# First batch of an FFT mixer: the way back to tokens through DRAM instead of through transposes, and three sections of batch 2 ahead of the first unit

## The chip, the cores and the metric

The kernel runs on one core of a Trainium2 chip. The metric is device time in microseconds (us) for one execution of the whole program. The kernel before takes 1328.95 us, the median of 3 runs (1328.45 to 1333.54).

## What is computed

The input x has 4 batches of 3136 tokens with 256 channels. First a filter in the frequency domain runs along the tokens, then two blocks of dense layers:

```python
y = irfft(rfft(x, axis=1) * (filt_r + 1j * filt_i), n=3136, axis=1)
h = (y^T @ U @ V)^T                      # rank 32, along the tokens
u = y + h
r = u + relu(u @ w_ch1) @ w_ch2          # 256 -> 1024 -> 256
n = (r - mean(r)) / sqrt(var(r) + 1e-6) * g_ln
out = r + relu(n @ w2_ch1) @ w2_ch2      # again 256 -> 1024 -> 256
```

All inputs are fp32 and the result is wanted to fp32 accuracy, so each dense product is made of several products of split operands (high and low parts).

## The kernel before

The transform of 3136 = 112 x 28 points is done in two stages of small matmuls with tables, forward, then a multiplication with the filter, then two stages back. The last stage back and the addition of the rank-32 term are made together, in 28 **units** of 448 tokens (`unit(i)`, seven to a batch). A unit reads a tile `wt` with rows of the third stage's result and a tile `ic` with table columns, and leaves 448 tokens, channels on partitions, in the split tiles `ah` and `al`. Units feed 25 **blocks** of 512 tokens. A block has a phase "a" (`m1` at L824, `m2` at L843 to L845: first dense pair) and a phase "b" (`m1` at L824, `m2` at L851, L852: second pair). A phase has 8 steps, each an `m1` of six matmuls and an `m2` of an earlier step. The loop over `steps` (L1211) also calls units when they are due, conversions of weights (`pr`), and pieces of the transform of batches 2 to 4 (the generator `rest`, from step `FFT0` on, first stage not before step `FFT1`).

Batch 1 is transformed on its own ahead of the first step, by the class `First`, with its data in the SBUF tile `big` (channels on partitions). `columns()` works through 14 channel groups of frequencies, one in a turn of its loop: four transposes out of `big` (`psz`, L656), the second stage (`ps2`, L670), the filter (`filtered`, on DVE and, for all groups but one, POOL) and the third stage (`ps3`, L681). That third stage has the data as the stationary operand and a table beside a slice of U as the moving one, 144 columns wide, so its result has channels on partitions: `spill` (ACT) copies it back into `big`, and `project` (DVE) sums up the 32 columns that belong to U. Behind the loop `mixed()` turns that sum by two transposes (L705), and `part(u)` turns the data for unit u by eight transposes (L728) and two copies (ACT, L732 on DVE). For units 0 to 3 (`DIRECT = 4`) the result goes straight into `wt`; for 4 to 6 it is stored to the DRAM tensor `bd[0]` (L734), from which `load_unit` reads it. Parts 0 and 1 run ahead of the first step, parts 2 to 6 in the steps 0, 1, 2, 5 and 6 (`PARTS`).

Batches 2 to 4 go another way (`fft(b)`): the first stage in seven sections (`load1`, `stage1`, L301) with its result in DRAM (`zd`), then for seven groups the second stage, filter and third stage (`back`, L373 and L375), here with the table stationary in 64x64 quarters of the array, so that tokens are on partitions. The result goes to DRAM (`bd`), and the product with U (`pt`, L381) is made by matmuls of its own. A unit of such a batch loads its rows in two halves (`load_unit`, L756) and uses the two-halves form (L801, L806) instead of the form for `DIRECT` units (L786, L788).

The order of the instructions on every engine is the order in which this program writes them. All transfers but a few leave through one queue, SP's, in that order. A transfer on SP waits there until its data and its target are free, and what stands behind it waits too. Each transfer also waits for the one eight places ahead of it to land, since eight completion counters are used in turn.

Of the kernel before, what the change touches and what calls it, by code (L numbers as in the profile page):

```python
# [10 lines left out]
F32 = mybir.dt.float32  # L11
# [28 lines left out]
SLOTS, UAHEAD = 4, 2  # L40
# [4 lines left out]
DIRECT = 4  # L45

PARTS, UPARTS = (0, 1, 2, 5, 6, 8), 10
# [13 lines left out]
def _tables():  # L61
# [75 lines left out]
    parted = np.zeros((2, P, 2, PP))  # L137
    for g in range(2):
        for k in range(2):
            parted[0, g * 64:(g + 1) * 64, k] = d[0, k * 64:(k + 1) * 64]  # L140
            parted[1, g * 64:(g + 1) * 64, k] = d[1 - g, k * 64:(k + 1) * 64]
    turn = np.zeros((P, NM, QT))
    for h in range(2):
# [9 lines left out]
        "c_d32": np.ascontiguousarray(parted.transpose(1, 0, 2, 3).astype(np.float32)),  # L153
# [5 lines left out]
        "c_inv": np.ascontiguousarray(inv.transpose(1, 0, 2).astype(np.float32)),  # L159
# [24 lines left out]
def fft_mixer_kernel(ctx: ExitStack, tc: tile.TileContext, x, U, V, flt, w1, w2, gln, w1b, w2b,  # L184
                     c_fwd32, c_d32, c_e32, c_p32, c_s1, c_s2, c_s3, c_inv, c_half, c_w, out):
# [94 lines left out]

    def fft(b):
# [12 lines left out]
        def stage1(t):  # L294
# [99 lines left out]
        def finish():  # L394
            t = pt.pop(b)
            s = [flat(fp.tile([P, 2, D], F32, tag="xs", name="tt", bufs=2))[0:R].rearrange("p (a q) -> p a q", q=D) for _ in range(2)]
            for a in range(1, 4):
                acopy(s[a // 2][:, a % 2], t[a * R:(a + 1) * R])
            nc.vector.tensor_tensor(out=s[0][:, 0], in0=t[0:R], in1=s[0][:, 1], op=ALU.add)
            nc.vector.tensor_tensor(out=s[1][:, 0], in0=s[1][:, 0], in1=s[1][:, 1], op=ALU.add)  # L400
            nc.vector.tensor_tensor(out=s[0][:, 0], in0=s[0][:, 0], in1=s[1][:, 0], op=ALU.add)
            stack(b, s[0][:, 0].rearrange("p (q k) -> p k q", k=KT))

# [39 lines left out]
        finish()  # L443
        yield 0

    class First:
# [3 lines left out]
        def load(self, conversions):  # L450
# [5 lines left out]
            for j in range(NM // 4):  # L456
# [17 lines left out]
                for _ in range(FETCHES.count(j)):  # L474
# [75 lines left out]
        def u_half(self, h):  # L550
# [8 lines left out]
            ps = outer("pst")  # L559
# [13 lines left out]
        def u_parts(self):  # L573

            held["uh"] = const.tile([P, 2 * SLOTS * (PP + R)], F32, tag="uh", name="uh_sb")[:, :NG * R].rearrange("p (g r) -> p g r", r=R)
# [26 lines left out]

        def columns(self):


            zt, ys, n, w = {}, {}, NCH, PP + R
            d0, d1 = self.d
            self.t = d1[:, 2, 0:KT * 2 * R].rearrange("p (h g r) -> p h g r", h=KT, g=2)
            turns = [self.u_half(h) for h in (1, 0)]

            def slot(i):
                return d1[:, 0:2] if i == 0 else d0[:, i % SLOTS]

            def spill(pvs, i):
                for g, pv in enumerate(pvs):
                    a = (2 * i + g) * PP
                    (acopy if i or g == 0 else nc.vector.tensor_copy)(self.big[:, :, a:a + PP], pv[:, :, :PP])

            def project(pvs, i):
                for g, pv in enumerate(pvs):  # L620
                    acc = self.t[:, :, g]
                    if i == n - 1:
                        nc.vector.tensor_copy(acc, pv[:, :, PP:])
                    else:
                        nc.vector.tensor_tensor(out=acc, in0=pv[:, :, PP:], in1=acc, op=ALU.add)

            def filtered(i, ps):
# [10 lines left out]
                else:  # L638
                    yr = ps_t.tile([P, 512], F32, tag="t", name="yr").rearrange("p (a d) -> p a d", a=2)
# [8 lines left out]
            due = None  # L648
            for j in range(n + BACKL):
                if j < n:  # L650
                    i = n - 1 - j
                    ps = (ps_h if j % 2 else ps_t).tile([P, 512], F32, tag="h" if j % 2 else "t", name="psz")
# [6 lines left out]
                if due:  # L659
                    spill(*due)  # L660
                    project(*due)
                due = None
# [10 lines left out]
                if j >= BACKL:  # L673
                    i = n + BACKL - 1 - j
                    ya = ys.pop(i)
                    pvs = [outer("ps3")[:, :2 * w].rearrange("p (h w) -> p h w", w=w) for g in range(2)]
                    for dh in range(KT):
                        for k in range(2):
                            for g in range(2):
                                gs = slice(g * HALF, (g + 1) * HALF)  # L680
                                nc.tensor.matmul(pvs[g][:, dh], dealt(ya[gs, k], dh), slot(i)[gs, k], start=k == 0, stop=k == 1)  # L681
                    due = pvs, i
# [3 lines left out]
                if j == 1:  # L686
                    for k in range(2):
                        nc.gpsimd.tensor_copy(d0[:, 1:, k, 0:PP], d0[:, 0, k, 0:PP].unsqueeze(1).to_broadcast([P, SLOTS - 1, PP]))
                for i in (n - 1, n - 2) if j == BACKL - 1 else (n + BACKL - UAHEAD - 1 - j,) if BACKL <= j < n + BACKL - UAHEAD else ():
                    acopy(slot(i)[:, :, PP:w], self.uq[:, :, i])  # L690
                yield j
            spill(*due)
            project(*due)

        def mixed(self):

            tt = fp.tile([P, 2, D], F32, tag="xs", name="tt", bufs=2)[:, 0]
            ps = ps_t.tile([P, 512], F32, tag="t", name="pst")
            for dh in range(KT):
                acc = self.t[:, dh]  # L700
                nc.vector.tensor_tensor(out=acc[:, 0], in0=acc[:, 0], in1=acc[:, 1], op=ALU.add)
            yield
            for dh in range(KT):
                acc = self.t[:, dh]
                nc.tensor.transpose(ps[:R, dh * P:(dh + 1) * P], acc[:, 0], ident)  # L705
            yield
            acopy(tt[0:R], ps[:R, :D])
            stack(0, tt[0:R].rearrange("p (k q) -> p k q", k=KT))

        def part(self, u, between=None):  # L710

            m = slice(UW * u, UW * u + UW)
            if u < DIRECT:
                wt[u] = new_unit(u)
            for dh in range(KT):
                ds = slice(dh * P, (dh + 1) * P)
                if u < DIRECT:
# [9 lines left out]
                for k in range(UW):  # L727
                    nc.tensor.transpose(ps[:PP, k * P:(k + 1) * P], v[:, :, UW * u + k], ident)  # L728
# [538 lines left out]
```

## Time and profile before

| | us |
|---|---|
| median of 3 runs | 1328.95 |
| profiled execution | 1325.22 |
| its span, first to last instruction | 1323.4 |
| TensorE (PE) busy | 1305.7 (99%) |
| VectorE (DVE) busy | 800.1 (60%) |
| ScalarE (ACT) busy | 429.1 (32%) |
| GpSimd (POOL) busy | 151.7 (11%) |

The profiled execution lies 3.7 us below the median of the runs and 1.8 us above its own span. A busy PE counts every matmul from its start to its modelled end, and matmuls overlap, so the length of a stretch of PE work is read from the start of one group to the start of the next, not from the sum of durations. [...]

### The profile page before, as it was taken

The page shows a single profiled execution, that of the slowest core. Times are in us where ns is not written, and L with a number is a line of the kernel's source. Part 1 is how long each engine was busy: PE and PEld are TensorE (multiplying, and loading weights), DVE is VectorE, ACT ScalarE, POOL GpSimd, SP SyncE. Part 2 cuts the span into 40 slices and gives each one's busy share as a digit, 9 for nine tenths or more (in the row PEclk, how much of TensorE's full clock was granted, in tenths as well). Part 3 has the DMA queues.
Part 4 walks back from the last instruction along what each step waited for, and adds up shares of the span by engine and source line. Part 5 has one row for each costly group of instructions (what it writes and reads, how often), then busy time and mean ns, then how long its engine had stood idle before and what let it go on. Part 6 is the DMA issues. An engine that isn't in the chain of part 4 may idle for free.

```text
span 1323.4 us, 22450 instructions
## 1 busy us (share of the span) xinstructions
PE 1305.7 (99%) x8606; PEld 1041.8 (79%) x8606; DVE 800.1 (60%) x1643; ACT 429.1 (32%) x857; POOL 151.7 (11%) x133
## 2 busy tenths in 40 slices
PE   9999999999999999999999999999999999999998
PEld 8688678777778787787777877878888888888887
DVE  6867976666565666556655575665555545455454
ACT  4656432333323323223222233232222223222222
POOL 2845520212000001000001010000000000000000
PEclk9999999999999999999999999999999999999999
DMA  8734365675563446344555464422202211210111
GB/s 252 197 101 137 90 190 183 169 197 160 157 207 91 123 124 173 104 136 110 143 164 147 127 170 121 122 70 66 50 20 62 66 32 52 66 49 5 44 49 40
DMA packets 166531, 151.15 MB, mean 114 GB/s; under 512 B 65912, under 2 KB 142568, under 8 KB 166424
## 3 DMA queue, kind: packets, MB, share of 16 engines
q1 hardware_dynamic: 166120, 148.25, 40.4%
q0 software_dynamic: 304, 1.47, 0.5%
q8 instruction: 68, 1.11, 0.4%
q14 instruction: 39, 0.32, 0.1%
HBM read 91.10 MB, written 47.54 MB: 105 GB/s over the span
## 4 chain that ended last, share of the span: by engine, by line
PE 87%; DVE 5%; DMA 3%; POOL 1%; ACT 1%; issue 1%; SPq 1%; POOLq 0%; DVEq 0%; ACTq 0%
PE psh L824 38%; PE pso L851 13%; PE pso L852 7%; PE pso L843 6%; PE pso L844 6%; PE pso L845 6%; PE psu L801 2%; PE ps L301 2%; PE ps L375 1%; PE ps L341 1%; PE psu L806 1%; PE pt L381 1%; DVE hl L828 1%; DMA stg<-v 1%; DMA x<-x 1%
## 5 line engine op out<-in xcount | busy, mean ns | idle before, releaser
L828 DVE SCALAR_TENSOR_TENSOR hl<-psh,hh 128x512 fp32r<-128x512 f32 (+1 forms) x400 | 271.6, 680 | 363.0 <-ACT hh L827 361.8
L827 ACT ACTIVATE hh<-psh 128x512 fp32r<-128x512 f32 (+1 forms) x400 | 235.1, 589 | 655.8 <-PE psh L824 655.6
L851 PE MATMUL pso<-wb,hh 128*128 128x512 f32 x784 | 285.0, 397 | 0.8 <-DVE x L866 0.4
L824 PE MATMUL psh<-ah,wb 128*128 128x512 f32 (+1 forms) x800 | 280.0, 391 | 0.6 <-DVE hl L828 0.6
L852 PE MATMUL pso<-wb,hl 128*128 128x256 f32 x784 | 219.7, 280 | 0.5 <-DVE hl L828 0.5
L824 PEld LDWEIGHTS psh<-ah,wb 128*128 128x128 f32 x800 | 149.7, 188 | 46.4 <-issue 5.7
L851 PEld LDWEIGHTS pso<-wb,hh 128*128 128x128 f32 x784 | 147.3, 188 | 36.3 <-DVE x L866 1.6
L824 PE MATMUL psh<-ah,w1h 128*128 128x512 f32 (+1 forms) x400 | 158.2, 396 | 0.0
L844 PE MATMUL pso<-hl,w2h 128*128 128x512 f32 (+1 forms) x400 | 154.4, 386 | 2.7 <-DVE hl L828 2.7
L843 PE MATMUL pso<-hh,w2h 128*128 128x512 f32 (+1 forms) x400 | 155.8, 390 | 0.4 <-DVE x2t L891 0.3
L824 PE MATMUL psh<-al,wb 128*128 128x512 f32 (+1 forms) x400 | 155.4, 389 | 0.0
L824 PE MATMUL psh<-al,w1h 128*128 128x512 f32 (+1 forms) x400 | 155.2, 388 | 0.0
L852 PEld LDWEIGHTS pso<-wb,hl 128*128 128x128 f32 x784 | 147.9, 189 | 8.3 <-DVE hl L828 0.9
L824 PE MATMUL psh<-ah,w1l 128*128 128x512 f32 (+1 forms) x400 | 154.4, 386 | 0.0
L845 PE MATMUL pso<-hh,w2l 128*128 128x512 f32 (+1 forms) x400 | 154.0, 385 | 0.0
L357 POOL TENSOR_TENSOR xs<-xs,ft 128x512 f32<-128x512 f32 x42 | 56.2, 1337 | 645.6 <-DMA xs<-zc 375.8
L824 PEld LDWEIGHTS psh<-ah,w1h 128*128 128x128 f32 x400 | 75.1, 188 | 22.7 <-issue 4.7
L891 DVE SCALAR_TENSOR_TENSOR x2t<-pso,ln,x2t 128x256 f32<-128x256 f32 x196 | 89.8, 480 | 3.7 <-PE pso L852 0.3
L843 PEld LDWEIGHTS pso<-hh,w2h 128*128 128x128 f32 x400 | 75.1, 188 | 20.5 <-issue 5.4
L844 PEld LDWEIGHTS pso<-hl,w2h 128*128 128x128 f32 x400 | 75.2, 188 | 18.3 <-DVE hl L828 3.9
L824 PEld LDWEIGHTS psh<-ah,w1l 128*128 128x128 f32 x400 | 75.2, 188 | 15.9
L845 PEld LDWEIGHTS pso<-hh,w2l 128*128 128x128 f32 x400 | 75.1, 188 | 15.1
(150 smaller groups left out, 1333.9 us busy)
## 6 DMA issues: line engine op xcount, KB each, us to landing
ft<-flt SPq DMA_DIRECT2D x42, 512.0 KB
xd<-x SPq DMA_DIRECT2D x96, 128.0 KB
x2t<-xd SPq DMA_DIRECT2D x24, 512.0 KB
wt<-bd SPq DMA_DIRECT2D x48, 224.0 KB
out<-x2t SPq DMA_DIRECT2D x84, 128.0 KB
xs<-zc SPq DMA_DIRECT2D x168, 64.0 KB
xt<-x SPq DMA_DIRECT2D x84, 112.0 KB
zd<-ze SPq DMA_DIRECT2D x84, 112.0 KB
```

The lines of the kernel that those rows point to most:

```text
L301: nc.tensor.matmul(pss[j][quarter(h), m * D:(m + 1) * D], ct[rows56(j), 2 * h + m], xs[h][rows56(j), m], start=True, stop=True)
L357: nc.gpsimd.tensor_tensor(out=xs, in0=xs, in1=fi[:, e], op=ALU.mult)
L801: nc.tensor.matmul(pss[h][c * HALF:(c + 1) * HALF, dh, h * spare + m:h * spare + half:UW], t[rows, m, d0:d0 + HALF], ic[rows, m, :], start ...
L824: nc.tensor.matmul(ps[:, :n], w[:, kt, fs], a[:, kt, :n], start=j == 0, stop=j == 3 * KT - 1)
L827: nc.scalar.activation(out=hh[:, :n], in_=ps[:, :n], func=AF.Relu)
L828: nc.vector.scalar_tensor_tensor(out=hl[:, :n], in0=ps[:, :n], scalar=0.0, in1=f32(hh[:, :n]), op0=ALU.max, op1=ALU.subtract)
L843: nc.tensor.matmul(o, wh[:, f, ds], hh[:, :n], start=f == 0, stop=False)
L844: nc.tensor.matmul(o, wh[:, f, ds], hl[:, :n], start=False, stop=False)
L845: nc.tensor.matmul(o, wl[:, f, ds], hh[:, :n], start=False, stop=f == FT - 1)
L851: nc.tensor.matmul(o, hh[:, cs], w, start=f == 0, stop=False, skip_group_check=True)
L852: nc.tensor.matmul(o[:, D:], hl[:, cs], w[:, :D], start=False, stop=f == FT - 1, skip_group_check=True)
L891: nc.vector.scalar_tensor_tensor(out=o, in0=acc[c][:, half * D:(half + 1) * D], scalar=rs[:, c:c + 1], in1=o, op0=ALU.mult, op1=ALU.add)
```

## The change

- The third stage of batch 1 takes the form of the other batches: the table is stationary, in quarters, for two groups at once (`back(p)`, seven calls). Tokens lie on partitions; the product with U is accumulated in `pt[0]` by four matmuls of 32 columns for each call. Two ACT copies bring the result to a free part of `big`, and four transfers store it to `bd[0]`.
- `spill`, `project`, `mixed`, all transposes of `part`, the table copies on POOL (L688) and the slices of U beside the table (L690) go away. The sum over U's rows is finished by `finish(0)`, as for the other batches.
- All seven units of batch 1 load their rows from `bd[0]` and take the two-halves form.
- The transform of batch 2 starts in `columns()` (`FILLJ`): the loads of its first section stand in turn 13, those of the second in turn 14. Between `finish(0)` and unit 0 stand three sections of its first stage (`FILL = 3`), which leave their result in `big`.
- Some tiles move between PSUM banks.

```diff
-SLOTS, UAHEAD = 4, 2
 PACE = 4
 VSTEP = 11
-DIRECT = 4
-
-PARTS, UPARTS = (0, 1, 2, 5, 6, 8), 10
+FILL, FILLJ = 3, 13
+
+WBSTEP, UPARTS = 2, 10
...
-                ze = four(F32, "fev", "ze")
+                ze = first.spare(t, e) if b == 1 and t < FILL else four(F32, "fev", "ze")
...
-            self.d = [const.tile([P, 2 * SLOTS * (PP + R)], F32, tag="uh", name="d32").rearrange("p (s k q) -> p s k q", k=2, q=PP + R),
-                      fp.tile([P, 2 * (D + R)], F32, tag="fev", name="d32", bufs=2).rearrange("p (s q) -> p s q", q=PP + R)]
-            nc.sync.dma_start(self.d[0][:, 0, :, 0:PP], c_d32[:, 0])
-            nc.sync.dma_start(self.d[1][:, 0:2, 0:PP], c_d32[:, 1])
+            self.d = const.tile([P, NG * R], F32, tag="uh", name="d32")[:, :8 * HALF].rearrange("p (v k j q) -> p v k j q", v=2, k=2, j=2)
+            nc.sync.dma_start(self.d, c_d32)
...
+        def bank(self, j, name):
+            return ps_o.tile([P, 512], F32, tag=f"o{j}", name=name, bufs=1)
+        def spare(self, t, e):
+            return self.big[:, e, 512 * t:512 * t + 512]
...
-            def spill(pvs, i):
...
-            def project(pvs, i):
...
-                    yr = ps_t.tile([P, 512], F32, tag="t", name="yr").rearrange("p (a d) -> p a d", a=2)
+                    yr = self.bank(3, "yr").rearrange("p (a d) -> p a d", a=2)
...
-            due = None
+            def back(p):
+                ya = [ys.pop(2 * p + s) for s in range(2)]
+                pss = [self.bank(g, "ps3") for g in range(2)]
+                for s in (1, 0):
+                    for k in range(2):
+                        for g in range(2):
+                            gs = quarter(g)
+                            for h in range(2):
+                                nc.tensor.matmul(pss[g][quarter(h), s * D:(s + 1) * D], self.d[gs, 0 if p or s else 1, k, h], ya[s][gs, k],
+                                                 start=k == 0, stop=k == 1)
+                if p == n // 2 - 1:
+                    pt[0] = ps_t.tile([P, 512], F32, tag="t", name="pt")[:, :D]
+                for s in (1, 0):
+                    for k in range(2):
+                        q = 2 * s + k
+                        nc.tensor.matmul(pt[0][q * R:(q + 1) * R], self.uq[:, k, 2 * p + s], ya[s][:, k], start=p == n // 2 - 1, stop=p == 0)
+                to = bd[0].rearrange("(j a s g p) w -> a g j p s w", j=2, a=n // 2, s=2, g=2)[p]
+                for g in range(2):
+                    at = BLK * (6 + (p + 1) % 2)
+                    be = self.big[:, g, at:at + BLK]
+                    acopy(be.rearrange("p (s k q) -> p s k q", s=2, k=KT), pss[g].rearrange("p (s q k) -> p s k q", s=2, k=KT))
+                    for h in range(2):
+                        nc.sync.dma_start(to[g, h], be[rows56(h)].rearrange("p (s w) -> p s w", s=2))
...
-                    ps = (ps_h if j % 2 else ps_t).tile([P, 512], F32, tag="h" if j % 2 else "t", name="psz")
+                    ps = self.bank(2 + j % 2, "psz")
...
-                if j >= BACKL:
...
+                if j > BACKL and (j - BACKL) % 2:
+                    back((n + BACKL - j) // 2)
...
-                if j == 1:
...
-        def mixed(self):
...
-        def part(self, u, between=None):
...
-        rows, n, table = (PP, PP, c_inv) if i < DIRECT else (P, QT, c_half)
-        ic = mp.tile([P, UW * PP], F32, tag="ic", name="ic")[:rows, :UW * n].rearrange("p (m q) -> p m q", q=n)
-        nc.sync.dma_start(ic, table[:, m0:m0 + UW])
-        return t[:PP] if i < DIRECT else t, ic
+        ic = mp.tile([P, UW * PP], F32, tag="ic", name="ic")[:, :UW * QT].rearrange("p (m q) -> p m q", q=QT)
+        nc.sync.dma_start(ic, c_half[:, m0:m0 + UW])
...
-        rows = bd[b].rearrange("(h q m) w -> h q m w" if b else "(q h m) w -> h q m w", h=2, m=NM)
+        rows = bd[b].rearrange("(h q m) w -> h q m w", h=2, m=NM)
...
-        if i < DIRECT:
...
+            for _ in range((5, 1)[j - FILLJ] if FILLJ <= j < FILLJ + 2 else 0):
+                want = next(rest)
+        finish(0)
+        state = [want, -9]
...
-            while loaded <= min(i, NUNIT - 1) and loaded // UPB in tstk and (loaded >= UPB or loaded < stored):
+            while loaded <= min(i, NUNIT - 1) and loaded // UPB in tstk:
...
-        later = leftover()
+        load_to(1)
+        for t in range(FILL):
+            for _ in range(2):
+                want = next(rest)
+            for act in todo.pop(0):
+                act()
+        state[0] = want
+        nc.gpsimd.dma_start(s2_sb, c_s2)
+        nc.gpsimd.dma_start(s3_sb, c_s3)
         units_to(need(0))
...
-                if idx in PARTS:
-                    next(later, None)
+                if idx == WBSTEP:
+                    leftover()
```

Two places show how the order moves. The first is SP's queue from the last weights of the columns on. Before (`ic` are the tables of units 0 to 3, `stg` weights to convert, `bd_115` is `bd[0]`):

```order
L601 DMA f_828<-flt 32x256 x4
L960 DMA stg<-w 128x2x512
L748 DMA ic<-c_inv 112x448 x4
L960 DMA stg<-w 128x2x512
L734 DMA bd_115<-wt_1176 112x4x128
```

With the change (`xt` and `ct` are the data and table of a section of batch 2, `zd_85` takes that section's result; the stores from `big` to `bd_115` are the last three calls of `back`):

```order
L655 DMA bd_115<-big 56x2x256 x4
L299 DMA xt<-x 56x512 x4
L301 DMA ct<-c_s 128x256
L655 DMA bd_115<-big 56x2x256 x4
L299 DMA xt<-x 56x512 x4
L301 DMA ct<-c_s 128x256
L655 DMA bd_115<-big 56x2x256 x4
L695 DMA ic<-c_half 128x224
L703 DMA wt<-bd_115 56x1024 x2
L695 DMA ic<-c_half 128x224
L703 DMA wt<-bd_115 56x1024 x2
L299 DMA xt<-x 56x512 x4
```

The next row there is the table `ct` of the third section. So units 0 and 1 read `bd[0]` behind the last four stores to it, and the data of the third section stand behind these reads.

The second place is PE between the last third stage and the first `m1`. Before:

```order
L728 MATMUL psw<-ident,big 112x128 x4
L705 MATMUL pst<-ident,d_188 32x128 x2
L728 MATMUL psw<-ident,big 112x128 x12
L786 MATMUL psu<-ic,wt 128x112 x4
L788 MATMUL psu<-v_sb,tk 128x448
L786 MATMUL psu<-ic,wt 128x112 x4
```

With the change (of the last section only its last two rows; the rows of `xt` are eight matmuls a section):

```order
L648 MATMUL pt<-hl,uq 32x256 x2
L648 MATMUL pt<-ya,uq 32x256 x2
L310 MATMUL ps_1026<-xt,ct 64x256
...
L310 MATMUL ps_1078<-xt,ct 64x256
L310 MATMUL ps_1079<-xt,ct 64x256
L737 MATMUL psu<-ic,wt 64x56 x32
L742 MATMUL psu<-v_sb,tk 128x256 x4
L737 MATMUL psu<-ic,wt 64x56 x32
L742 MATMUL psu<-v_sb,tk 128x256 x4
L760 MATMUL psh<-ah,w1h 128x512
```

Three sections now stand between the columns and unit 0, in an order that PE keeps, and the transposes are gone here as well as in the steps behind.

## Rows read from the trace of the kernel before

**Rows 1.** The page, part 1: busy us, share of the span, instructions of each engine.

```profile
PE 1305.7 (99%) x8606; PEld 1041.8 (79%) x8606; DVE 800.1 (60%) x1643; ACT 429.1 (32%) x857; POOL 151.7 (11%) x133
```

**Rows 2.** Stretches: length, busy us per engine (PE, PEld, DVE, ACT, POOL), PEclk, DMA share, GB/s.

```profile
28.30:73.50 45.20, 41.70 (x398) 28.67 (x398) 36.98 (x80) 27.10 (x78) 40.06 (x44) 1.00 0.76 197
73.50:80.50 7.00, 6.46 (x55) 6.38 (x56) 4.22 (x11) 4.21 (x10) 0.00 (x0) 1.00 0.10 29
80.50:140.00 59.50, 59.50 (x295) 49.44 (x294) 46.38 (x73) 36.59 (x70) 29.30 (x23) 1.00 0.39 117
140.00:170.00 30.00, 26.28 (x114) 18.23 (x113) 29.36 (x41) 12.92 (x23) 19.56 (x15) 1.00 0.43 101
```

**Rows 3.** Timeline of PE, columns and behind: start, us, instructions, [idle before <-releaser].

```profile
48.48 1.26 PE L681 MATMUL ps<-d,hl 64*128 64x144 f32 x16
49.67 0.65 PE L656 MATMUL psz<-ident,big 128*112 128x128 f32 x4
...
72.08 1.38 PE L681 MATMUL ps<-d,ya 64*128 64x144 f32 x16 [0.29 <-DVE d L625]
...
80.49 0.40 PE L824 MATMUL psh<-ah,w1h 128*128 128x512 f32 x1
```

**Rows 4.** Timeline of PE, starts of steps 8 and 9.

```profile
108.83 0.40 PE L824 MATMUL psh<-ah,w1h 128*128 128x512 f32 x1
...
111.57 0.39 PE L824 MATMUL psh<-ah,w1h 128*128 128x512 f32 x1
```

**Rows 5.** Timeline of PE later: section, unit and third stage of batches 2 to 4.

```profile
174.37 1.09 PE L301 MATMUL ps<-xt,ct 56*64 56x256 f32 x16
175.39 0.50 PE L824 MATMUL psh<-ah,wb 128*128 128x512 f32 x1
...
201.87 1.15 PE L801 MATMUL psu<-ic,wt 56*64 56x56 f32 x64
...
203.53 0.40 PE L824 MATMUL psh<-ah,wb 128*128 128x512 f32 x1
...
258.40 1.11 PE L375 MATMUL ps<-ya,s_sb 64*64 64x256 f32 x16
259.44 0.64 PE L381 MATMUL pt<-ya,uh_sb 128*32 128x256 f32 x8
260.01 0.50 PE L824 MATMUL psh<-ah,wb 128*128 128x512 f32 x1
```

**Rows 6.** Who PE waited for: us in total, times, longest; columns, then 82 to 200 us.

```profile
PE ps L681 <- DVE d L625: 1.1, 2, 0.8
...
PE pso L844 <- DVE hl L828: 2.7, 3, 1.5
```

**Rows 7.** Timeline of ACT: one 512-wide copy out of PSUM, and pieces of unit 1.

```profile
66.45 0.60 ACT L219 ACTIVATE z<-psz 112x512 f32<-112x512 f32 x1 [1.54 <-PE psz L656]
...
79.59 0.22 ACT L219 ACTIVATE ah<-psu 128x64 fp32r<-128x64 f32 x1 [0.56 <-PE psu L788]
80.11 0.81 ACT L219 ACTIVATE ah<-psu 128x384 fp32r<-128x384 f32 x2 [0.29 <-DVE al L222]
```

**Rows 8.** Timeline of SP's queue: start, us of issuing, transfers.

```profile
171.92 1.66 SPq L290 DMA_DIRECT2D xt<-x  x4
...
1222.40 2.18 SPq L919 DMA_DIRECT2D xd<-x  x4
1226.93 0.38 SPq L925 DMA_DIRECT2D x2t<-xd  x1
```

**Rows 9.** The chain that ended last, by time: start, us, what; a unit's load.

```profile
105.82 2.87 DMA wt<-bd
```

**Rows 10.** The page, part 6: a transfer, KB, us from issue to landing.

```profile
s_sb<-c_s POOLq DMA_DIRECT2D x1, 64.0 KB, 2.3
```

**Rows 11.** Timeline of PE at the start: the same matmul, first and second burst.

```profile
1.06 5.07 PE L1116 MATMUL warm<-ones 128*128 128x128 f32 x22 [1.06 <-DVE ones L1112]
...
7.93 2.41 PE L529 MATMUL warm<-ones 128*128 128x128 f32 x20
```

More of the change, by code (lines that the diff above doesn't have):

```diff
@@ L279, in stack, with finish @@
         sub(tk[R:2 * R], t, f32(tk[0:R]))
+    def finish(b):
+        t = pt.pop(b)
+        s = [flat(fp.tile([P, 2, D], F32, tag="xs", name="tt", bufs=2))[0:R].rearrange("p (a q) -> p a q", q=D) for _ in range(2)]
+        for a in range(1, 4):
+            acopy(s[a // 2][:, a % 2], t[a * R:(a + 1) * R])
+        nc.vector.tensor_tensor(out=s[0][:, 0], in0=t[0:R], in1=s[0][:, 1], op=ALU.add)
+        nc.vector.tensor_tensor(out=s[1][:, 0], in0=s[1][:, 0], in1=s[1][:, 1], op=ALU.add)
+        nc.vector.tensor_tensor(out=s[0][:, 0], in0=s[0][:, 0], in1=s[1][:, 0], op=ALU.add)
+        stack(b, s[0][:, 0].rearrange("p (q k) -> p k q", k=KT))
     def fft(b):
@@ L392, in back @@
                     defer(0, lambda c=c, to=to, be=be: nc.sync.dma_start(to[c], be[rows56(c)]))
[L394 to L402, printed above, removed]
         load1(0)
@@ L558, in u_half @@
             yield
-            ps = outer("pst")
+            ps = ps_h.tile([P, 512], F32, tag="h", name="pst")
             a = 0 if h else R
@@ L672, in columns @@
                     filtered(i, ps)
-                if j >= BACKL:
[L674 to L682, printed above, removed]
+                if j > BACKL and (j - BACKL) % 2:
+                    back((n + BACKL - j) // 2)
                 if j in UTURN:
@@ L685, in columns @@
                 self.filters(j + AHEAD)
-                if j == 1:
[L687 to L690, printed above, removed]
-                yield j
-            spill(*due)
-            project(*due)
@@ L695, in mixed @@
-        def mixed(self):
[L697 to L708, printed above, removed]
@@ L780, in split @@
             sub(lo, src, f32(hi))
-        if i < DIRECT:
-            for dh in range(KT):
-                ps = ps_h.tile([P, 512], F32, tag="h", name="psu")
-                for m in range(UW):
-                    nc.tensor.matmul(ps[:, m:UN:UW], t[:, m, dh * P:(dh + 1) * P], ic[:, m, :],
-                                     start=m == 0, stop=False, skip_group_check=True)
-                nc.tensor.matmul(ps[:, :UN], lows(dh), vs[:, :, m0 * QT:m0 * QT + UN // 2].rearrange("p h (s m) -> p s h m", m=UW),
-                                 start=False, stop=True, skip_group_check=True)
-                for k, done, off, n in pieces():
-                    split(acth[k][:, dh, off:off + n], actl[k][:, dh, off:off + n], ps[:, done:done + n])
-            return
         pss = [ps_h.tile([P, 512], F32, tag="h", name="psu").rearrange("p (d n) -> p d n", d=KT) for _ in range(2)]
@@ L1140, in fft_mixer_kernel @@
                 load_v()
-        mixed = first.mixed()
-        next(mixed)
-        for u in range(2):
-            first.part(u, mixed if u == 0 else None)
-            next(mixed, None)
-        rest = chain()
-        state = [0, -9]
+            for _ in range((5, 1)[j - FILLJ] if FILLJ <= j < FILLJ + 2 else 0):
+                want = next(rest)
+        finish(0)
+        state = [want, -9]
         def advance(idx, ph, f):
@@ L1191, in leftover @@
         def leftover():
-            nonlocal stored
-            for u in range(2, UPB):
-                first.part(u)
-                stored = max(stored, u + 1)
-                yield
             wb = const.tile([P, 4, KT * FF], F32R, tag="wb", name="wb")
```

65 lines of the change are left out of this document (12 added, 53 removed).

## The prediction

> **What bounds the kernel now.** I read the page first, then the stretches, then the timelines of the engines where the change works. PE is busy for 99% of the span [rows 1], so any matmul added or saved counts, unless it stands beside a stall. The stretches [rows 2] show where stalls are. In the columns of batch 1 (28.3 to 73.5 us) PE is busy 41.7 of 45.2 us, POOL 40.1, and the transfers take a share of 0.76 of the DMA engines. Between columns and first step (73.5 to 80.5) hardly a transfer runs. From 80.5 to 140 PE has no gap. From 140 to 170 DVE is full (29.4 of 30.0) and PE lacks 3.7 us, waiting for DVE [rows 2, 6]. [...]
>
> So the change has three places: the columns, the turn from columns to first step, and the steps behind. T is the end of the last third stage; before, T = 72.08 + 1.38 = 73.46, and the first `m1` starts at 80.49 [rows 3], 7.0 us later.
>
> **Columns.** Removed: 14 third stages of 48.48 to 49.67 = 1.19 us [rows 3], 16.7 us. Added: quarters, which batches 2 to 4 run already, eight matmuls in 258.40 to 259.44 = 1.04 us, so 14 x 1.04 = 14.6; and the product with U, four matmuls in 0.57 us (259.44 to 260.01), seven times, 4.0 [rows 5]. That is +1.9. Gone is PE's wait for DVE's `project`, 1.1 us [rows 6]. On ACT two copies of 512 columns a pair take the place of four of 224, and the slices of U go; POOL loses its copies of the table. These stand beside PE work, so I cost them at nothing; if that cover failed, PE would wait for `z` copies on ACT, 0.60 us each [rows 7]. Filter loads are queued behind the new stores, but were written three turns ahead; nothing too, with the exception in the second rival. Sum: **+0.8 us**, T near 74.3.
>
> **The turn.** This is the part with a new wait, and I follow it from T on.
> - ACT copies two banks, 2 x 0.60 [rows 7]. SP is by then still issuing the loads of the second section, since they stand behind the stores of the call before, whose copies end at about T - 2.65 + 1.2 (the last call takes 2 x 1.04 + 0.57 = 2.65). Two stores of those and five loads, at 1.66 / 4 = 0.42 each [rows 8], end at T + 1.5; the last four stores are issued by T + 3.1.
> - A store followed at once by its reader shows the landing: the last issue ends at 1222.40 + 2.18 = 1224.58, the read goes at 1226.93 [rows 8]: 2.35 us. So the reads of unit 0 go at T + 5.5.
> - SP then issues unit 0's two halves, a table, unit 1's two halves, and only behind them the four loads and the table of the third section: ten transfers, 4.1 us, T + 9.6. The table lands 2.3 (64 KB) to 2.9 us later [rows 9, 10]; I take 2.6, T + 12.2, since it lies between in size.
> - PE keeps its order. It has U's product and two sections to do, some 2.7 us, then stands until T + 12.2, although unit 0's rows arrive at about T + 9.2. Then come the third section, 1.02 us (174.37 to 175.39), two units of 1.66 us (201.87 to 203.53) [rows 5], and the last pieces of unit 1 on ACT (0.22, 0.41, 0.22) and one on DVE of about the first's length [rows 7]: in all T + 17.6. Before, this took 7.0, so **+10.6 us**.
> - The clock. No row here has a gap of 6 us. The nearest row is the start: after idling, 22 records of a matmul take 5.07 us, and 20 of the same 2.41 us later [rows 11], so 22 would be 2.65; a cold start costs 2.4 us. The bounds are 0 and 2.4; I take **+2.4**, as the gap is nearer to that row than to the gaps of 1.5 us or less, behind which 1.00 stands. The clock column itself reads 1.00 even at the start, so the row shows slow matmuls, not their cause.
>
> [...]
>
> **The steps behind.** Steps 0 to 7 take 80.49 to 108.83 = 28.3 us [rows 3, 4], with five parts and two direct units in them. A plain step is 111.57 - 108.83 = 2.74 us [rows 4]. Steps 0 and 1 lack their `m2`, so seven plain steps and two units of the new form are 19.2 + 3.3 = 22.5 us: **-5.8 us**. Three sections no longer run later: 3 x 1.02 [rows 5], **-3.1 us**. Units 2 and 3 now come from DRAM; their reads stand on SP behind 22 more transfers of sections, about T + 21, and unit 2 is due at about T + 20 + 8, so I cost this at nothing; were it late, PE would wait at step 4. Parts 0 and 1, `mixed` and the two direct units ahead of step 0 are inside the 7.0 us. The stall from 140 to 170 us depends on DVE's work a step, which the change leaves alone there: nothing. The transform of batch 2 is three sections ahead from then on; later PE has hardly a gap to fill by that: nothing.
>
> **Sum.** 0.8 + 10.6 + 2.4 - 5.8 - 3.1 = +4.9 us on a profiled execution of 1325.2, which lies 3.7 us below the median. On the median: 1328.95 + 4.9 = 1333.9, say **1334 us**. A measurement of this kernel can tell some 0.5% from no change, 6.6 us; the forecast is inside.
>
> **Rivals.**
> - *The clock holds through the gap.* For it: 1.00 in every stretch here. Against: the start row. +2.5 us, 1331.5. Chance 0.15.
> - *The DMA engines become the bound, in the columns and the turn: slower.* The columns move 197 GB/s x 45.2 us = 8.9 MB at a share of 0.76 [rows 2]. The change adds 28 stores of 112 KB and eight section loads of 112 KB with two tables, 4.3 MB, to the same stretch; at the same cost a byte the share would be 1.13, 13% of 45 us = 5.9 us over. Then filter loads are late in the columns, or the last stores land late and everything behind them with them. That gives up to +10.8, 1339.8; past +6.6 it decides the sign, so as soon as 1.7 of the 5.9 us reach PE. Against it: before, the third stage's waits name DVE and no transfer [rows 6], and the stretch behind the columns, with a share of 0.10 [rows 2], can take what is left over. Chance 0.33.
> - *The turn is short.* If the cold start costs nothing, the third section's data come at T + 9 (-3.2), and DVE, relieved in steps 0 to 7, has no stall from 140 on (-3.7): 2.5 - 3.2 - 3.7 = -4.4, 1324.5. To be faster by over 6.6 us the reads would have to land with hardly any wait, which rows 8 and 9 speak against. Chance 0.12, half of it beyond 0.5%.
> - *The forecast*, 0.40.
>
> **How the numbers follow.** From the forecast, the first rival and half of the third: within 0.5% 0.58. Slower by over 0.5%: the second rival and the edge of the forecast, 0.36. Faster: 0.06. The range from 1325 (the third rival, nearly whole) to 1341 (the second at its full price) leaves out some 2 in 10.
>
> **What would show it.** In the profile after: quarters and U's product at 1.04 and 0.57 us; T between 73.5 and 76; a gap of PE of 5 to 9 us before the third section, ended by a transfer of `xt` or `ct` and not of `wt`; the first `m1` 17 to 21 us after T; slower matmuls behind the gap; steps of 2.74 us from then on with only two units in them; steps 20 to 28 still waiting for DVE. Wrong I am if the first `m1` starts within 14 us of T, or if PE waits in the columns for filter data.

## The result and the profile after

The changed kernel takes 1347.25 us (median of 4 runs, 1346.69 to 1348.87), the kernel before 1328.7 us beside it: a ratio of 1.0136, 95% interval 1.0108 to 1.0165. It is slower by some 18 us, and the prediction (1334, range 1325 to 1341) missed that. The profiled execution took 1348.87 us, 1.6 above its median, with a span of 1347.1; that of before lay 3.7 below its own. So the traces are 23.7 us apart, where the medians are 18.5 apart. One of the runs below, of third_first, took 1605.72 us at a mean granted clock of 0.748 and isn't counted in its median.

The page, part 1, and the stretches (columns as in [rows 2]), of the kernel after; the last line is the same stretch of the kernel before:

```profile
PE 1308.4 (97%) x8804; PEld 1033.7 (77%) x8804; DVE 794.8 (59%) x1608; ACT 424.1 (31%) x825; POOL 150.8 (11%) x131
```

```profile
28.30:73.50 45.20, 41.62 (x453) 22.37 (x446) 32.70 (x55) 25.65 (x52) 38.63 (x43) 1.00 0.82 233
73.50:80.50 7.00, 0.84 (x16) 0.20 (x12) 1.57 (x4) 3.01 (x7) 1.32 (x2) 0.90 1.01 235
80.50:104.50 24.00, 12.97 (x185) 9.61 (x185) 5.41 (x10) 3.60 (x8) 0.00 (x0) 0.50 0.79 230
104.50:110.00 5.50, 5.50 (x13) 4.13 (x14) 2.53 (x6) 1.09 (x2) 0.00 (x0) 0.51 0.24 74
...
200.00:300.00 100.00, 96.11 (x674) 72.35 (x673) 65.24 (x142) 31.88 (x62) 13.12 (x10) 0.98 0.65 182
```

```profile
200.00:300.00 100.00, 100.00 (x752) 75.74 (x751) 65.36 (x143) 32.06 (x65) 13.04 (x10) 1.00 0.63 181
```

PE works as much in the columns as it did [rows 2]. From 73.5 to 104.5, 31 us, it works 13.8. In that stretch the transfers, which before took a share of 0.10 in its first 7 us [rows 2], take a share of 1.01 and 0.79 of the DMA engines at 230 to 235 GB/s, and PE's granted clock falls: 0.90 up to 80.5, 0.50 up to 104.5, 0.51 up to 110. The last two rows show 3.9 us without PE work between 200 and 300 us, where before had none.

The timeline of PE (columns as in [rows 3]) shows which instructions wait:

```profile
72.50 1.23 PE L641 MATMUL ps<-ya,d 64*64 64x256 f32 x14
...
80.46 1.99 PE L310 MATMUL ps<-xt,ct 56*64 56x256 f32 x16 [6.16 <-DMA ct<-c_s]
83.75 2.08 PE L310 MATMUL ps<-xt,ct 56*64 56x256 f32 x16 [1.30 <-DMA ct<-c_s]
93.75 2.10 PE L310 MATMUL ps<-xt,ct 56*64 56x256 f32 x16 [7.91 <-DMA ct<-c_s]
...
104.47 0.80 PE L760 MATMUL psh<-ah,w1h 128*128 128x512 f32 x1 [0.78 <-ACT ah L218]
...
118.39 0.50 PE L760 MATMUL psh<-ah,w1h 128*128 128x512 f32 x1 [1.10 <-ACT ah L218]
...
131.48 0.40 PE L760 MATMUL psh<-ah,w1h 128*128 128x512 f32 x1
```

T, the end of the third stage, is 72.50 + 1.23 = 73.73. Each of the three sections waits for its table `ct`: the first for 6.16 us, the third for 7.91. A section, 16 records for its eight matmuls, takes about twice its time (1.99 to 2.10 us from start to end, for 1.09 in [rows 5]). The first `m1` starts at 104.47, T + 30.7; step 8 starts at 131.48.

The timeline of SP's queue (columns as in [rows 8]) tells why the tables are late:

```profile
68.04 2.67 SPq L299 DMA_DIRECT2D xt<-x  x4
70.76 1.43 SPq L301 DMA_DIRECT2D ct<-c_s  x1
72.29 2.09 SPq L655 DMA_DIRECT2D bd<-big  x4
78.94 2.21 SPq L299 DMA_DIRECT2D xt<-x  x4
81.19 0.37 SPq L301 DMA_DIRECT2D ct<-c_s  x1
81.66 1.71 SPq L655 DMA_DIRECT2D bd<-big  x4
83.42 0.40 SPq L695 DMA_DIRECT2D ic<-c_half  x1
85.14 0.75 SPq L703 DMA_DIRECT2D wt<-bd  x2
...
87.23 1.67 SPq L299 DMA_DIRECT2D xt<-x  x4
89.13 0.35 SPq L301 DMA_DIRECT2D ct<-c_s  x1
```

Between the issues that end at 74.4 and 78.94 SP issues nothing. What it waits for stands in its own waits (us in total, times, longest), and how long that takes in the chain (start, us, what):

```profile
SPq L299 <- DMA xt<-x: 5.2, 2, 4.5
```

```profile
68.94 11.00 DMA xt<-x
...
82.56 2.51 DMA bd<-big
...
89.13 4.52 DMA ct<-c_s
```

A load of the first section, issued at 68.94, lands at 79.94, 11 us later; the one issued ahead of it lands at 78.88. These two stand eight places ahead of the second section's first two loads on SP (its 1003 transfers in this trace signal eight semaphores in turn): the first of those goes at 78.94 and the next at 79.96, 0.06 and 0.02 us after the landings, and behind them stand the last four stores, whose data ACT had copied by 74.5. A store lands in 2.51 us, near the forecast's 2.35; the stores are only issued at 81.66 to 83.37. The third section's table then takes 4.52 us to land, where the forecast had 2.6.

The transfers of 60 to 105 us (totals, then one transfer: KB, us from issue to landing), after:

```profile
DMA packets 7214, 10.58 MB, mean 235 GB/s; under 512 B 1084, under 2 KB 4403, under 8 KB 7210
v_sb<-vd POOLq DMA_DIRECT2D x1, 1176.0 KB, 11.2
```

and before:

```profile
DMA packets 3855, 5.30 MB, mean 118 GB/s; under 512 B 297, under 2 KB 2866, under 8 KB 3850
v_sb<-vd POOLq DMA_DIRECT2D x1, 1176.0 KB, 7.6
```

The load of V leaves POOL's queue at 67.6, beside the first section's loads on SP's, and itself takes 11.2 us instead of 7.6.

### The profile page after: what moved, and what is told of

Same layout as the page of the kernel before. It is cut to its first block, busy times and chain, and to the rows that moved or that the text cites. A ratio compares the mean times of both kernels' runs of the same rounds, so it can differ in the third digit from the quotient of the medians.

```text
span 1347.1 us, 22812 instructions
## 1 busy us (share of the span) xinstructions
PE 1308.4 (97%) x8804; PEld 1033.7 (77%) x8804; DVE 794.8 (59%) x1608; ACT 424.1 (31%) x825; POOL 150.8 (11%) x131
## 4 chain that ended last, share of the span: by engine, by line
PE 84%; DVE 5%; DMA 5%; ACT 2%; SPq 1%; issue 1%; POOL 1%; ACTq 0%; DVEq 0%; POOLq 0%
PE psh L760 37%; PE pso L787 13%; PE pso L788 6%; PE pso L779 6%; PE pso L780 6%; PE pso L781 6%; PE psu L737 2%; PE ps L310 2%; PE psu L742 1%; PE ps L384 1%; PE ps L350 1%; DVE hl L764 1%; DMA stg<-v 1%; PE pt L390 1%; DMA xt<-x 1%
## 5 line engine op out<-in xcount | busy, mean ns | idle before, releaser
L780 PEld LDWEIGHTS pso<-hl,w2h 128*128 128x128 f32 x400 | 75.2, 188 | 19.1 <-DVE hl L764 4.7
L760 PEld LDWEIGHTS psh<-ah,w1l 128*128 128x128 f32 x400 | 75.7, 189 | 16.1
```

Of the source, the lines that this page charges most:

```text
L760: nc.tensor.matmul(ps[:, :n], w[:, kt, fs], a[:, kt, :n], start=j == 0, stop=j == 3 * KT - 1)
L780: nc.tensor.matmul(o, wh[:, f, ds], hl[:, :n], start=False, stop=False)
```

## The experiments

Four explanations were on trial: **bytes** (A: too many go through the DMA engines around T), **order** (B: stores and third section's loads stand behind the wrong things on SP), **clock** (C), and **a slow way back** (D). All runs in one table; T, the first `m1` and step 8 are starts on PE's timeline (T an end), "rest" is the span from step 8 on. The kernel before ran beside each group of versions, at medians of 1328.18 to 1330.09 us, and the ratio is to that, so small differences between versions are read from the ratio.

| kernel | T | first m1 | step 8 | rest | median us | ratio to before (95%) |
|---|---|---|---|---|---|---|
| before | 73.5 | 80.5 | 108.8 | 1214.6 | 1328.7 | 1 |
| after | 73.7 | 104.5 | 131.5 | 1215.6 | 1347.25 | 1.0136 (1.0108 to 1.0165) |
| no_sections | 74.5 | 92.0 | 120.3 | 1215.8 | 1337.98 | 1.0069 (1.0053 to 1.0084) |
| stores_first | 75.4 | 104.9 | 133.0 | 1213.6 | 1347.14 | 1.0136 (1.0118 to 1.0154) |
| busy_gaps | 73.1 | 114.3 | 140.3 | 1215.8 | 1358.24 | 1.0219 (1.0204 to 1.0234) |
| less_in_turn | 76.2 | 101.4 | 129.0 | 1212.7 | 1342.88 | 1.0100 (1.0082 to 1.0118) |
| busy_half | 73.1 | 100.7 | 126.7 | 1213.4 | 1344.49 | 1.0124 (1.0102 to 1.0147) |
| back_less | 75.2 | 90.3 | 117.4 | 1216.9 | 1335.83 | 1.0048 (1.0033 to 1.0063) |
| back_busy | 75.3 | 92.9 | 120.4 | 1216.5 | 1337.88 | 1.0062 (1.0047 to 1.0077) |
| two_sections | 72.9 | 97.1 | 124.8 | 1214.1 | 1340.06 | 1.0082 (1.0067 to 1.0097) |
| act_first | 81.7 | 107.1 | 135.5 | 1212.8 | 1351.02 | 1.0173 (1.0156 to 1.0190) |
| third_first | 75.2 | 99.9 | 127.9 | 1215.0 | 1342.40 | 1.0108 (1.0091 to 1.0125) |
| act_less | 82.2 | 100.5 | 128.2 | 1214.0 | 1343.99 | 1.0116 (1.0101 to 1.0131) |
| two_less | 75.7 | 95.2 | 123.5 | 1214.8 | 1338.88 | 1.0060 (1.0042 to 1.0078) |

From the first `m1` to the end of the span all fourteen take 1239 to 1244 us, while the first `m1` itself moves by 34. To within 5 us, the time of a version is that of its first `m1`.

**no_sections**, the way back without sections ahead:

```diff
-FILL, FILLJ = 3, 13
+FILL, FILLJ = 0, 13
...
-            for _ in range((5, 1)[j - FILLJ] if FILLJ <= j < FILLJ + 2 else 0):
-                want = next(rest)
         finish(0)
-        state = [want, -9]
+        state = [0, -9]
...
```

> The changed kernel's way back alone: no section of batch 2 runs ahead of the first unit, and none is loaded in the columns. Theory A (bytes: the DMA engines are full from 66 to 104 us, and the turn is as long as what has to go through them): the eight section loads, two tables and the sections' stores leave the turn, the last stores land by T+6 beside the load of V, the units' reads by T+9, so the first m1 starts at 89 to 93 us instead of 104.5, the sections' 3.1 us come back in the steps, and the time is 1335 to 1339 us. Theory B (order: the last stores and the third section's loads only stand too far back in SP's queue; bytes cost nothing): stores issued by T+2, landed by T+4.4, first m1 at 85 to 88 us, 1331 to 1334 us. Theory D (the way back through DRAM is itself that long): first m1 at 98 us or later, 1344 us or more.

First `m1` at 92.0, 1338.0 us: as A has it, and neither B's 85 to 88 nor D's 98. SP's queue and the unit's start on PE:

```profile
67.02 10.68 SPq L655 DMA_DIRECT2D bd<-big  x12
77.75 0.40 SPq L695 DMA_DIRECT2D ic<-c_half  x1
80.23 0.75 SPq L703 DMA_DIRECT2D wt<-bd  x2
```

```profile
83.33 0.46 PE L737 MATMUL psu<-ic,wt 56*64 56x56 f32 x4 [8.28 <-DMA wt<-bd]
```

The last stores are out by T + 3.2, the reads go at T + 5.75 and the rows are there at T + 8.9: the prediction's own T + 3.1, T + 5.5 and T + 9.2. The first of these agrees by luck: the forecast got there with five loads of a section to issue, and here, without them, the last two stores wait for ACT's second copy, which starts only at 76.33 (T + 1.85), behind 1.55 us of waiting for earlier stores to land. On the ratios half of the loss, some 9 us, belongs to the way back, the other half, some 9 too, to three sections that were to gain 3.1.

**stores_first**, the last stores ahead of the second section's loads:

```diff
-            for _ in range((5, 1)[j - FILLJ] if FILLJ <= j < FILLJ + 2 else 0):
+            for _ in range(5 if j == FILLJ else 0):
                 want = next(rest)
+        want = next(rest)
         finish(0)
```

> The five loads of the second section are issued behind the last four stores instead of ahead of them; nothing else moves. Theory B (order): the last stores are issued by 76.5 us instead of 83.4, the reads of unit 0 go at 80 instead of 85.1, the third section's loads by 84 and the third section starts by 89 instead of 93.8; the first m1 starts near 98 us, and the time is 1340 to 1342 us. Theory A (bytes): the same bytes go through full engines, the stores land as late as now or the second section's data come later by as much; the first m1 stays within 2 us of 104.5, and the time at 1345 to 1349 us.

No change, so B in this form falls. SP stops about when it does in the changed kernel (73.7 to 78.3 us for the first stop), now ahead of the stores, and waits there for earlier transfers to land (4.5 us for a store, 1.3 for `xt`):

```profile
72.95 9.05 SPq L655 DMA_DIRECT2D bd<-big  x8
```

**less_in_turn**, less of V and no small tables in the crowd (`vv`, `vs_d`, `rest_of` and `vsd` are views of V's tile and of its source):

```diff
-        nc.gpsimd.dma_start(v_sb[:3 * R].rearrange("p (h n) -> p h n", h=2), vd.rearrange("h a r n -> (a r) h n"))
+        nc.gpsimd.dma_start(vv[:, :, :480], vs_d[:, :, :480])
+        nc.gpsimd.dma_start(vv[:, 0, N // 2 - 32:], vs_d[:, 0, N // 2 - 32:])
...
-        nc.gpsimd.dma_start(s2_sb, c_s2)
-        nc.gpsimd.dma_start(s3_sb, c_s3)
         units_to(need(0))
...
+        nc.sync.dma_start(f32(rest_of[:, :, 480:n - 32]), vsd[:, :, 480:n - 32])
+        nc.sync.dma_start(f32(rest_of[:, 1, n - 32:]), vsd[:, 1, n - 32:])
+        nc.sync.dma_start(s2_sb, c_s2)
+        nc.sync.dma_start(s3_sb, c_s3)
```

> Of V only the columns that the first two units read are loaded in the columns stage (381 KB); the other 795 KB and the two small tables s_sb (256 KB) are loaded behind the first units on SP's queue. Theory A (bytes): 1.05 MB less at 232 GB/s is 4.5 us; the first section starts at 76 to 77 us instead of 80.5, the first m1 at 99 to 101, and the time is 1341 to 1344 us. Theory B (order alone): SP's order up to the first units is unchanged, so the first section starts within 1 us of 80.5 and the time is 1346 to 1348 us.

4.4 us faster than the change, close to A's estimate of 4.5, although its columns ended 2.4 us later. The first section starts almost at once, the second 3 us sooner; the third still waits 7.7:

```profile
77.11 1.09 PE L310 MATMUL ps<-xt,ct 56*64 56x256 f32 x16 [0.38 <-DMA ct<-c_s]
80.55 2.42 PE L310 MATMUL ps<-xt,ct 56*64 56x256 f32 x16 [2.35 <-DMA ct<-c_s]
90.67 2.10 PE L310 MATMUL ps<-xt,ct 56*64 56x256 f32 x16 [7.70 <-DMA ct<-c_s]
```

V on POOL's queue and the section's loads on SP's were both slow while they ran side by side in the changed kernel (11.2 us for V, 11.0 for a load of the first section), and the section came sooner here, at 77.11 instead of 80.46, when V was smaller and the two tables were gone from there. Which of the two counted more, no run here shows.

**two_sections** (`FILL = 2`) and **third_first** (the third section's loads ahead of the units' reads) try what is left of B:

> Two sections ahead of the first unit instead of three; the loads of the third are still issued there, but PE doesn't wait for them. If the wait of 7.9 us for the third section's table is a wait of its own (its loads stand behind the units' reads), the units start when their rows land, at 88 to 90 us instead of 95.5; the first m1 is at 97 to 100, the third section's 1.0 us comes later, and the time is 1341 to 1343 us. If the units' rows land no earlier than that table, through the same full engines, the first m1 is at 102 or later and the time 1346 to 1348 us.

> The third section's five loads are issued ahead of the reads of units 0 and 1 on SP, not behind them; nothing else moves. If the wait of 7.9 us is one of order (its loads stand behind reads that wait for the stores to land): loads at 83.5 to 85.5 us, third section at 89 to 90 instead of 93.8, units' reads some 1 to 2 us later with their rows by 92; first m1 at 100 to 101.5, time 1343 to 1345 us. If the bytes set it, the rows are then late by as much as the section is early: first m1 at 103 or later, 1346 to 1348 us.

```diff
-        load_to(1)
         for t in range(FILL):
             for _ in range(2):
                 want = next(rest)
+            if t == 0:
+                load_to(1)
             for act in todo.pop(0):
```

Both came as a wait of its own would have it, first `m1` at 97.1 and 99.9; their times, 1340.1 and 1342.4 us, are each some 1 us below what was expected. Without the third section the units start when their rows are there (87.65, on PE's timeline of two_sections); with its loads ahead of the reads that section starts at 89.03 in place of 93.75, and the units right behind it:

```profile
87.65 0.47 PE L737 MATMUL psu<-ic,wt 56*64 56x56 f32 x4 [2.58 <-DMA wt<-bd]
```

```profile
89.03 2.24 PE L310 MATMUL ps<-xt,ct 56*64 56x256 f32 x16 [2.45 <-DMA ct<-c_s]
```

So the order on SP counts for the third section, and the first two cost little beside no_sections (1340.1 to 1338.0; the intervals of the ratios overlap).

**act_first**, the first section's loads on ACT's queue, to free SP of them (and the second's behind the last stores, with the edit of stores_first):

```diff
+        def queue(t):
+            return nc.scalar if b == 1 and t == 0 else nc.sync
...
-                    nc.sync.dma_start(xt[rows56(j)], xv[j, :, 4 * t + 2 * h:4 * t + 2 * h + 2])
+                    queue(t).dma_start(xt[rows56(j)], xv[j, :, 4 * t + 2 * h:4 * t + 2 * h + 2])
...
-            nc.sync.dma_start(tab[t], c_s1[:, 4 * t:4 * t + 4])
+            queue(t).dma_start(tab[t], c_s1[:, 4 * t:4 * t + 4])
...
```

> Three sections ahead as in the change, but the first section's five loads are issued by ACT's queue, and the second's on SP behind the last stores (as stores_first). Theory B2 (SP's queue stops because a transfer that it issued some eight before has not landed: the transfers it waited for were the first section's xt, in the change ahead of the second section's loads, in stores_first ahead of the last stores): the last stores are issued by 77.8 us as in no_sections, unit 0's rows are read at 81 instead of 85.1, the third section's loads go by 84, it starts at 89 to 90 instead of 93.8, and the time is 1342 to 1344 us. Theory A alone (full engines): the stores land late all the same, first m1 within 2 us of 104.5, 1345 to 1349 us.

A miss of both theories: 1351 us, slower than the change itself, with its first `m1` at 107.1. SP's stores wait for those loads although another queue issued them, and earlier, inside the columns; then the buffers in `big` come free late, ACT waits, and PE stands for 7.4 us ahead of the last third stages (SP's waits; timelines of ACT and of PE):

```profile
SPq L658 <- DMA xt<-x: 10.9, 2, 5.9
```

```profile
76.99 0.60 ACT L218 ACTIVATE big<-ps 128x512 f32<-128x512 f32 x1 [10.37 <-DMA bd<-big]
```

```profile
77.73 2.69 PE L644 MATMUL ps<-hl,d 64*64 64x256 f32 x16 [7.39 <-ACT big L218]
```

So the wait reaches from one of these queues to the other. Of SP's 10.9 us, 5.9 are for a load that ACT itself issued only at 66.11 and that landed at 68.25, and 5.0 for a slow one, issued at 67.42 and landed at 74.88. That B2's wait exists is shown; how much it costs beside the full engines is not, since no run has the one without the other.

**busy_gaps** and **busy_half** fill PE's waits with matmuls that nothing uses (`ones` by `ones` on a spare bank); busy_half has 27, 6 and 35 of them:

```diff
+        def busy(n):
+            for _ in range(n):
+                nc.tensor.matmul(idle[:, :P], ones, ones, start=True, stop=True)
...
         for t in range(FILL):
+            busy((55, 12, 70)[t])
```

> Adds 55, 12 and 70 matmuls of 128 x 128 on a spare bank ahead of the three sections, so that PE works in the three waits (6.2, 1.3 and 7.9 us). Theory C (the clock falls because PE stands still, and is a cost of its own): the granted clock stays at 1.00 in all stretches, a section takes 1.02 us instead of 2.0 to 2.1, a unit 1.7 instead of 3.1 and the first m1's matmuls 0.23 instead of 0.43 from start to start; the third section still waits for its table until 93.7, the first m1 starts near 101 and the time is 1339 to 1342 us. If the clock falls whatever PE does, or if its cost is hidden behind the transfers, 1346 us or more.

> As busy_gaps with half the matmuls (27, 6 and 35), since one took 0.227 us there: 6.1, 1.4 and 7.9 us, the length of the three waits. Theory C (the clock is a cost of its own): the sections start where they did (80.5, 83, 93.8), the granted clock holds through them, and what follows the third section's start takes 7.5 us to the first m1 as in busy_gaps instead of 10.7: first m1 near 101.3, and a little less behind it, 1342 to 1344 us. If the clock costs nothing here, 1346 to 1348 us.

busy_gaps missed, at 1358.2 us: one matmul took 0.227 us, twice what I had sized it by, so PE itself was late, with the first `m1` at 114.3. busy_half fits C in its first `m1` (100.7); its 1344.5 us lie just above the 1342 to 1344. Its stretches hold the clock until the first `m1`, and PE's timeline shows what follows the third section:

```profile
73.50:80.50 7.00, 7.00 (x71) 6.62 (x70) 1.57 (x4) 2.36 (x6) 0.66 (x1) 1.00 0.95 265
80.50:100.70 20.20, 16.15 (x258) 14.27 (x250) 5.38 (x10) 3.60 (x8) 0.00 (x0) 0.99 0.83 238
100.70:104.00 3.30, 3.30 (x8) 2.45 (x9) 1.12 (x3) 0.64 (x2) 0.00 (x0) 0.53 0.78 225
```

```profile
93.08 1.21 PE L310 MATMUL ps<-xt,ct 56*64 56x256 f32 x16 [1.62 <-issue]
...
95.04 1.14 PE L737 MATMUL psu<-ic,wt 56*64 56x56 f32 x60 [0.65 <-ACT zb L218]
...
97.91 1.14 PE L737 MATMUL psu<-ic,wt 56*64 56x56 f32 x60 [0.81 <-DVE al L221]
...
100.70 0.79 PE L760 MATMUL psh<-ah,w1h 128*128 128x512 f32 x1 [0.98 <-ACT ah L218]
```

From the third section to the first `m1` it takes 100.70 - 93.08 = 7.6 us instead of 104.47 - 93.75 = 10.7: at a granted clock of 0.99 instead of 0.50 it is 3.1 us shorter. The clock falls even so, to 0.53, behind the units, in and after which PE waits 0.65 to 0.98 us between groups, and the first `m1` is slow. On the medians the run is 2.8 us faster, but the intervals overlap.

**back_less** (no_sections with the smaller loads), **back_busy** (no_sections with 36 such matmuls), **two_less** (two_sections with the smaller loads) and **act_less** (act_first with two sections and the smaller loads):

> The way back alone (as no_sections) with the smaller load of V and the tables s_sb behind the first units (as less_in_turn). Theory A (bytes): the stores no longer share the engines with 1.05 MB, are issued by 75 to 76 us instead of 77.8 and landed 2 us sooner or more, the units' reads go at 77 to 78 instead of 80.2, the first m1 starts at 88 to 90 instead of 92.0, and the time is 1334 to 1336 us. If the way back is bound by SP's order and the landing alone, first m1 within 1 us of 92.0 and 1337 to 1339 us.

> The way back alone (as no_sections) with 36 matmuls of 128 x 128 (8.2 us) in the one wait of 8.3 us. Theory C: the clock stays at 1.00 up to the units, unit 0 to first m1 takes 6.6 us as in busy_gaps instead of 8.7, first m1 near 90, and 1 to 2.4 us are saved in the matmuls behind it: 1333.5 to 1335.5 us. If the clock costs nothing here, 1337 to 1339 us.

> Two sections ahead in the change's own order (two_sections, 1340.1 us) together with the smaller load of V and s_sb behind the units (less_in_turn, 4.4 us less than the change). If the two repairs add up: 1335 to 1337 us, the same as back_less (1335.8), which has no section ahead: then sections ahead give nothing even when their data come in time, since what they take from the transfers and give back near 280 us eats their 2 us. If they are worth their matmuls once nothing waits for them: 1334 us or less. If the V load and the third section cost the same microseconds: 1339 us or more.

> act_first with two sections instead of three, and with the smaller load of V and s_sb behind the units (less_in_turn): the shortest turn that all theories together give. First section by 77 us, second by 81, units' rows read at 80 to 81 and landed by 84 to 85; units at the lower clock 8.7 us, first m1 at 92.5 to 94, two sections (2 us) off the steps, 2 us given back near 280 us as in the other runs with sections ahead: 1335 to 1338 us, no better than back_less (1335.8). If sections ahead are worth their loads once nothing waits for them, 1333 us or less.

back_less came near what A has, 1335.8, first `m1` 90.3, though the last stores are out at 77.2 and not by 76: the best of the twelve, still behind before. back_busy missed: the granted clock held at 1.00 up to 88 us, but the rows arrived at 85.3 instead of 83.3, and from 88 to 92, in unit 1, it reads 0.62; its 1337.9 is where a clock without cost was to be, so that run doesn't show C. two_less (1338.9, ratio 1.0060) can't be told from back_less (1.0048), nor from two_sections (1.0082, the intervals overlap), and lies above the 1335 to 1337 of two repairs that add up. Its sections still wait for their tables, 1.03 and 2.61 us, so it shows no gain from sections ahead, but not what they would be worth with their data in time. act_less missed its 1335 to 1338 with the same kind of stop as act_first, 1344. No version beat the kernel before.

## Why the prediction was wrong

It is the sum of [rows 2] to [rows 11], step by step, on the traces:

- **Columns: right.** Forecast T near 74.3, measured 73.73 (before 73.46). PE has no wait for filter data; its waits for ACT's `z` copies, costed at nothing, are 2.6 us in place of 1.7. That the sum fits to 0.6 is in part luck: busy_gaps, busy_half, two_sections and third_first run the same program up to T, and theirs lies between 72.9 and 75.2.
- **The turn: the step that failed.** The prediction wrote that SP's issues "end at T + 1.5; the last four stores are issued by T + 3.1", and that PE has "two sections to do, some 2.7 us" from T on. This takes the loads of those sections as landed at T and prices an issue at 0.42 us whatever is under way. Measured: last stores issued by T + 9.6, reads at T + 11.4 (forecast 5.5), third section's loads out by T + 15.8 (9.6), its start T + 20.0 (12.2). That is +7.8 us: 6.2 in the issues, 1.6 in the landing of the table. The section on the kernel before names the wait for the transfer eight places ahead; the step left it out. no_sections, without the loads, keeps the forecast's times to 0.4 us (one of them by luck, see there). The wait that was forecast, ahead of the third section and ended by its table, came (7.91 us, forecast 5 to 9); the one of 6.16 ahead of the first section was not foreseen.
- **The tail of the turn.** From the third section to the first `m1` I took 5.4 us; at a granted clock of 0.99 it is 7.6 (busy_half): +2.2. Most of that are two waits that the sum lacked, 0.65 us of unit 0 for ACT's copy of the section's result and 0.81 of unit 1 for DVE's split of unit 0.
- **The clock: right in kind, mis-sized.** Forecast 2.4 us, measured 3.1 ahead of the first `m1` and 2.7 in steps 0 and 1 (104.47 to 109.92 is 5.45 us, for twelve matmuls that take 2.72 when they start 0.227 us apart, as at a granted clock of 1.00): +3.4. PE stood for 6.16, 1.30 and 7.91 us ahead of the sections, and the granted clock read 0.50 from 80.5 to 104.5.
- **Steps 0 to 7.** Forecast 22.5 us, measured 131.48 - 104.47 = 27.0. Less the 2.7 of clock, 1.8 remain: unit 2's result is wanted at once, and PE waits 1.10 us for ACT's copy and is slow again behind it.
- **The sections' -3.1 us.** From step 8 on the kernel takes 1215.6 us, before 1214.6. Seven runs with three sections ahead (after and six others) average 1214.1, between 1212.7 and 1215.8, three with none 1216.4: a gain of 2.3, and 1.8 of loss against before in those without. Half of that stands in steps 12 to 20, which take 25.3 us in all thirteen versions and 24.4 before; why stays open. The clock is another part: in nine of the thirteen the granted clock reads 0.50 for one or two more stretches of 3.4 us between step 8 and the last 4 us, in the kernel before for none; at half pace such a stretch costs up to 1.7 us (an estimate). One place of loss is plain: between 200 and 300 us PE lacks 2.2 to 3.9 us in all ten versions with sections ahead, 0.6 in the three without, and nothing before. The largest piece is a late `xs` near 285 us, for which DVE's `ya` waits, and `hl` stands behind `ya` on DVE (PE, DVE and POOL timelines of the kernel after, and the stretch behind the wait):

```profile
287.82 0.79 PE L760 MATMUL psh<-ah,wb 128*128 128x512 f32 x1 [2.44 <-DVE hl L764]
```

```profile
286.47 0.69 DVE L370 TENSOR_TENSOR ya<-ya,xs 128x512 f32<-128x512 f32 x1 [3.16 <-POOL xs L366]
```

```profile
285.18 1.26 POOL L366 TENSOR_TENSOR xs<-xs,ft 128x512 f32<-128x512 f32 x1 [3.02 <-DMA xs<-zc]
```

```profile
287.40:290.80 3.40, 2.98 (x7) 2.40 (x8) 2.16 (x4) 0.00 (x0) 0.00 (x0) 0.50 0.94 274
```

In the sum: -0.6 + 7.8 + 2.2 + 3.4 + 1.8 + 4.1 (from -3.1 to +1.0) = 18.7 us over the forecast on the traces; less 5.3 us by which the two profiled executions stand apart from their medians, 13.4, the miss of 1347.25 - 1333.9.

The second rival named the right thing (full DMA engines in the columns and the turn, late stores) and was priced at 5.9 us, as the overflow of bytes alone. It was the condition for the failed step, and less_in_turn, with 1.05 MB less there, gained 4.4 us: the lateness then passed through SP's order and its waits for loads (5.2 us in the changed kernel), the third section's wait and the clock.

## What to carry to other kernels

A load that is to be ready at a turn has to be priced at the rate that the DMA engines have left there, not at its landing time in a quiet stretch; here, with a share of 0.8 or more, a load took 11 us, where the prediction had taken 2.3 to 2.9 from quieter stretches. And one slow load can stop a queue, stores on the critical path too: here SP issued nothing from 74.4 to 78.94 us, until a load that stood eight transfers ahead had landed, and the four last stores went out only at 81.66 to 83.37. A filler has to be priced by what it needs on the full resource: a section saved 1 us of PE and brought 0.6 MB of loads, some 2.5 us of the engines at 232 GB/s (an estimate from the rates of 230 to 235 above).

## What was not expected of the hardware

PE's clock fell behind the units too, where PE had worked with no break over 1.62 us up to their start: in busy_half it is 0.53 from 100.7 to 104 behind waits of 0.65, 0.81 and 0.98 us. In no_sections it is 0.81 in the mean from 102 to 110, with matmuls 0.40 to 0.43 us apart from 106.94 to 110.33 instead of 0.23, shortly behind one wait of 1.10 at unit 2. In the changed kernel the same wait (118.39) leaves the granted clock at 1.00 from 117 to 120, yet the first two matmuls behind it start 0.56 and 0.34 us apart instead of 0.23; why stays open. In busy_half the clock, with matmuls of no use in PE's waits, read 0.99 from 80.5 to 100.7, through 20 us of waiting for data, but did not hold across the units.
